# A fused attention and mixture-of-experts kernel: the first expert's weight loads, one gather and a scatter pace moved in the queue, and score units issued in pairs

## The chip, the cores and the metric

The kernel runs on one core of a Trainium2 chip. A core has a matrix engine (TensorE, PE in the profile; its weight loads are PEld), a vector engine (VectorE, DVE), a scalar engine (ScalarE, ACT), GpSimd (POOL) and a sync engine (SyncE, SP), each with its own instruction queue, and 16 DMA engines that all queues share. The metric is the time of one execution in device microseconds; several executions are timed and their median is given.

## What is computed

The reference is a block-causal attention whose output goes through a noisy top-2 router and eight experts. It is cut here to what matters.

```
q, k, v: (8, 8, 576, 64)                       # batch, heads, sequence, head size
scores = q @ k.T / 8, masked where block(i) < block(j), blocks of 64
attn   = softmax(scores) @ v                   # per batch and head
x      = attn, heads side by side              # (4608 tokens, 512)
noisy  = x @ w_gate + log(1 + exp(x @ w_noise)) * noise      # (4608, 8)
top2   = the two largest experts of each token, softmax weights of the two
for each expert e and each token that chose it:
    out[token] += weight * (relu(x[token] @ w1[e]) @ w2[e])  # 512 -> 1024 -> 512
```

## The kernel before

**Attention in units.** The eight batches are taken in four groups `g` of two batches (`NG = 4`). A group has two sets `st` of four heads, and a set is cut into 13 score units (`UN = 13`), so that a group has 26 (`UG = 26`) and the kernel 104. `score_unit(g, u)` (line 285) issues one unit: a few matmuls of K against Q into one of two PSUM buffers `sc` (line 299; the two batches of the group lie in the two halves of the 128 rows), and one ScalarE exponential of 128x1024 elements into `esc` (line 302). The thirteenth unit of a set is small (lines 310 and 313) and is followed by memsets of the masked blocks (line 316).

**The slot table.** All other work is entered by hand in a table, `at(slot, fn, ...)`, and `run(slot)` issues what stands at a slot, sorted by kind: router steps, AV tiles, transposes, then everything else in the order of entry. In the attention stage slot `u` follows unit `u`:

```
    for u in range(NG * UG):
        score_unit(*divmod(u, UG))
        run(u)
```

The slots hold: `transpose_qk` (lines 256 and 259, Q and K of this and of the next group, copied out by DVE or ACT), `av_tile` (lines 341 and 352; probabilities times V into `av`, then a reciprocal and a multiply on DVE into `xr`, lines 356 and 357), `x_transpose` (line 373), the 16 router steps of a group (lines 381 to 478, DVE mostly), loads of Q, K, V and weights, and the scatters. An AV tile has an index `idx` of 0 to 8. Indices 0 to 7 are whole 128-token blocks; index 8 holds the last 64 tokens of both batches, with five terms `jt` for each head of which the last (`jt = 4`) has 64 rows only. Slots 104 to 110 finish the last group; from slot 111 on every slot follows one step of the expert stage.

**Scatters.** `scatter(g, j)` (line 496) writes 128 rows of a group's tokens, with their routing records, to the expert's place in DRAM (`xd`, one per half; groups 0 and 1 are half 0, groups 2 and 3 half 1). A group has 18 of them, on POOL. Each also waits for the last compute instruction issued before it (`pace[-1]`), which spreads them over time. Group 0's start at slot 52, one a slot; group 1's at 78, one a slot; group 2's at 101 and group 3's at 118, five in four slots.

**POOL's queue.** POOL issues the loads of V (line 212), of Q and K (lines 202 and 207) and of weights (line 232), the scatters, the gathers and the scatters of results, in the order in which the table names them. In the built program every DMA of POOL waits for one of eight semaphores in turn, so that the ninth waits for the first to land.

**Experts.** A half's tokens for an expert are a block of 640 places; the order of the blocks `b` is `SEQ`: experts 0, 1, 2 of half 0, experts 0, 1, 2 of half 1, then the halves in turn for experts 3 to 7. `load_x(b)` (line 516, issued by SP) reads a block transposed from `xd`, after all 36 scatters of its half have landed: `load_x(0)` into `xa`, the others into one of three buffers `xg`. `layer1(b, fb)` (line 571, eight per block, ReLU at line 574) and `layer2(b, c)` (line 583, five per block) follow. Steps are ordered `layer1(b, ...)`, the first `layer1` of the next block, then `layer2(b, ...)`. Block 0 thus takes slots 111 to 124, block 1 slots 125 to 137, and `layer1(3, 0)`, the first step that needs half 1, is at slot 145. `load_x(3)` is issued after slot 138's step, `layer1(2, 1)`.

After `layer2` ACT writes the weighted result to `yd` (lines 588 and 590). For a token's second expert `gather(b, c)` (line 611, POOL) fetches the first result from `yd`, DVE adds the two (line 593), and POOL scatters the sum to `out` (line 595). Block 0 gathers nothing, block 1 has one gather, issued after `layer1(1, 2)`, at slot 126.

**Weights.** `load_w(wE, 0, k)` loads expert 0 in four pieces of 512 KB at slots 46 to 49; expert 1 comes at slots 80, 84, 88 and 92, expert 2 from slot 112 on.

Of the kernel before, what the change touches and what calls it, by code (L numbers as in the profile page):

```python
# [19 lines left out]
def kernel(  # L20
# [37 lines left out]
    LT = (0, 1, 2, 3, 3, 4, 5, 5)  # L58
    BIG = float(1 << 20)
    SET = 4  # L60
# [3 lines left out]
    UG = 2 * UN  # L64
# [32 lines left out]
    wE = main.enter_context(tc.tile_pool(name="wE", bufs=2))  # L97
# [117 lines left out]
    def v_loads(g):  # L215
        return [(load_v, g, idx) + r for idx in range(TG) for r in token_rows(g, idx)]
# [107 lines left out]
    def av_tile(g, st, idx, part=None):  # L324
        esc, esc4 = escs[(g, st)]
        vb = vt[g % 2]
        if g not in xrs:
            xrs[g] = xr_pool.tile([P, TG, DR], BF16, tag="xr", name="xr")
            nc.gpsimd.memset(xrs[g][:, :, Dm + 2 * NREC:DR], 0.0)
            nc.gpsimd.tensor_copy(xrs[g][:, :, Dm + 4:Dm + 6].bitcast(I32)[:, :, 0], tokm[:, g, :])  # L330
        xr = xrs[g]
        if part != 1:
            avs_open[idx] = av_ps.tile([P, SET, D + 1], F32, tag="av", name="av")
        av = avs_open[idx]
        for hh in (range(SET) if part is None else range(2 * part, 2 * part + 2)):
            h = st * SET + hh
            if idx < 8:
                hf, ib = divmod(idx, 4)
                for jt in range(ib + 1):
                    c = EO[jt] + (ib - jt) * P  # L340
                    nc.tensor.matmul(out=av[:, hh, :], lhsT=esc[:, hh, hf, c:c + P],  # L341
                                     rhs=vb[:, 4 * hf + jt, h, :], start=(jt == 0), stop=(jt == ib))
            else:
                for jt in range(5):
                    for hf in range(2):
                        sl = slice(64 * hf, 64 * hf + 64)
                        if jt < 4:
                            c = EO[jt] + (4 - jt) * P
                            lhsT, rhs = esc[:, hh, hf, c:c + 64], vb[:, 4 * hf + jt, h, :]
                        else:  # L350
                            lhsT, rhs = esc4[sl, hh, :], vb[sl, 8, h, :]
                        nc.tensor.matmul(out=av[sl, hh, :], lhsT=lhsT, rhs=rhs,
                                         start=(jt == 0), stop=(jt == 4))
        if part != 0:
            rden = small.tile([P, SET, 1], F32, tag="rden")
            nc.vector.reciprocal(rden, av[:, :, D:D + 1])
            ins = nc.vector.tensor_tensor(  # L357
                out=xr[:, idx, st * SET * D:(st + 1) * SET * D].rearrange("p (h d) -> p h d", h=SET),
                in0=av[:, :, 0:D], in1=rden.to_broadcast([P, SET, D]), op=ALU.mult)
            if g == NG - 1 and st == 1:  # L360
                pace.append(ins.ins.name)
# [244 lines left out]
    def gather(b, c):  # L606

        half, e = SEQ[b]
        yg = ffn["yg"][len(gathers) % GB]
        gathers.append(b)  # L610
        ins = nc.gpsimd.indirect_dma_start(  # L611
            out=yg, out_offset=None, in_=yd[half][0:e * CAP, :],
            in_offset=bass.IndirectOffsetOnAxis(ap=orows[half][:, e, c:c + 1], axis=0),
            bounds_check=e * CAP - 1, oob_is_err=False)
        tc.add_manual_dep(ins.ins, pace[-1], SYNC_DEP, reason="spreads the descriptors over time")
        ygs[(b, c)] = yg

    gathers = []
    GJ = (2, 3, 4, 6, 7)
# [3 lines left out]
    SEQ = [(0, e) for e in range(3)] + [(1, e) for e in range(3)]  # L623
# [5 lines left out]
    def at(slot, fn, *args):  # L629
        todo.setdefault(slot, []).append((fn, args))  # L630
# [94 lines left out]
    for g in range(NG):  # L725
        s0 = g * UG
        last = g == NG - 1

        for nm, ch, i in (("q", 1, 0), ("k", 1, 2), ("k", 2, 4), ("q", 2, 6), ("k", "4A", 7), ("q", "4A", 8),
                          ("q", 3, 10), ("k", 3, 12)):  # L730
            at(s0 + i, transpose_qk, g, nm, ch)
        if not last:
            for nm, ch, i in (("q", 0, 14 if g else 19), ("k", 0, 17 if g else 22), ("q", "4B", 22), ("k", "4B", 21)):
                at(s0 + i, transpose_qk, g + 1, nm, ch)
            for i, (fn, *a) in enumerate(v_loads(g + 1)):
                at(s0 + 9 + i, fn, *a)
        if g == 0:
            at(s0 + 13, load_qk, 1, (2,))
            at(s0 + 16, load_qk, 1, (3,))
        if g == 0:  # L740
            for i, t in enumerate(((0, 6, 5), (1, 5), (6, 9))):
                at(s0 + 20 + 4 * i, load_tiles, 2, "q", *t)
                at(s0 + 21 + 4 * i, load_tiles, 2, "k", *t)
        elif g == 1:
            at(s0 + 14, load_tiles, 3, "q", 0, TG)
            at(s0 + 17, load_tiles, 3, "k", 0, TG)
        for i, a in enumerate((15, 16, 17, 18, 18, 19, 20, 21, 22, 23)):
            at(s0 + a, av_tile, g, 0, *((i,) if i < 8 else (8, i - 8)))
        r0 = s0 + UG
        if not last:  # L750
            avs = (0, 1, 1, 3, 4, 4, 5, 6, 7, 8)
            xts_ = (3, 5, 7, 9, 10)
        if g < 2:
            rsl = (11, 11, 12, 13, 14, 15, 16, 17, 19, 20, 21, 22, 23, 24, 25, 26)
            r1 = 26
        elif g == 2:
            rsl = (11, 11, 12, 13, 13, 14, 15, 16, 18, 19, 19, 20, 20, 21, 22, 22)
            r1 = 23
        else:
            avs, xts_ = (0, 0, 1, 1, 2, 2, 3, 3, 4, 4), (2, 3, 4, 5, 5)  # L760
            rsl = (5, 6, 6, 7, 7, 8, 8, 9, 10, 10, 11, 11, 12, 12, 13, 13)
            r1 = 14
        for i in range(TG + 1):
            at(r0 + avs[i], av_tile, g, 1, *((i,) if i < 8 else (8, i - 8)))
        for j in range(5):
            at(r0 + xts_[j], x_transpose, g, j)
        for j in range(RSTEPS):
            at(r0 + rsl[j], router_step, g)
        for j in range(2 * TG):
            at(r0 + r1 + (j if g < 2 else 4 * j // 5), scatter, g, j)  # L770
    at(3, setup_consts)
    at(4, sort_nz, 0)
    at(8, transpose_nz, 0)
# [6 lines left out]
    at(UG + 4, clear_x, 0, UG + 3)  # L780
    at(2 * UG + 4, clear_x, 1, 2 * UG + 3)
    for k in range(4):
        at(2 * UG - 6 + k, load_w, wE, 0, k)
        at(3 * UG + 2 + 4 * k, load_w, wE, 1, k)
    for u in range(NG * UG):
        score_unit(*divmod(u, UG))
        run(u)
        if u == 3 * UG + 13:
            raws_up.close()
            ffn["x"] = raws_up.enter_context(tc.tile_pool(name="xgp", bufs=3, side="right", reuse_waits="tile"))  # L790
            ffn["rec"] = raws_up.enter_context(tc.tile_pool(name="recp", bufs=1, side="right", reuse_waits="tile"))
            wM = raws_up.enter_context(tc.tile_pool(name="wM", bufs=1, side="right", reuse_waits="tile"))
            at(3 * UG + 18, load_x, 0)
            at(3 * UG + 19, load_x, 1)
            at(3 * UG + 20, load_rec, 0)
            at(3 * UG + 21, load_x, 2)
            for k in range(4):
                at(4 * UG + (8, 10, 13, 16)[k], load_w, wM, 2, k)
# [32 lines left out]
    for fn, b, j in steps:  # L831
        fn(b, j)
        if fn is layer1:
            if (b, j) in XL:
                load_x(XL[b, j])
            if (b, j) == (2, 1):
                load_rec(1)
            if (b, j) == (3, 3):
                read_rec(1)
            if (b, j) in WL:  # L840
                load_w(*WL[b, j])
            if b < 9 and j in GJ and GJ.index(j) < LT[SEQ[b][1]]:
                gather(b, GJ.index(j))
            if 9 <= b + 1 < NB and j in GS and GS.index(j) < LT[SEQ[b + 1][1]]:
                gather(b + 1, GS.index(j))
        if fn is layer2 and 9 <= b + 1 < NB and j == 0 and LT[SEQ[b + 1][1]] > 4:
            gather(b + 1, 4)
            if b + 1 == NB - 1:
                nc.gpsimd.drain()  # L849
        run(slot)  # L850
        slot += 1
        open_top(slot)
# [8 lines left out]
    with tc.If(rs["over"] > 0):  # L861
# [16 lines left out]
        for half in range(NH):  # L878
            with tc.For_i(half * TH * P, (half + 1) * TH * P, P) as r0:
# [16 lines left out]
                for e in range(E):  # L896
# [3 lines left out]
                    for fb in range(FB):  # L900
                        hp = sc_ps.tile([P, 2, 512], F32, tag="sc")
                        for db in range(DB):
                            nc.tensor.matmul(out=hp[:, 0, 0:P], lhsT=w1sb[:, db, fb * P:(fb + 1) * P],
                                             rhs=xoT[:, db, :], start=(db == 0), stop=(db == DB - 1))
                        nc.scalar.activation(out=hsf[:, fb, :], in_=hp[:, 0, 0:P], func=AF.Relu)
                    yp = av_ps.tile([P, Dm], F32, tag="av")
                    for fb in range(FB):
                        nc.tensor.matmul(out=yp, lhsT=hsf[:, fb, :], rhs=w2sb[:, fb, :],
                                         start=(fb == 0), stop=(fb == FB - 1))
# [33 lines left out]
```

## Time and profile before

| what | value |
|---|---|
| median of 5 runs | 454.72 us (452.59 to 463.37) |
| profiled execution | 455.81 us, of which the span from the first to the last instruction is 453.9 us |
| mean granted TensorE clock | 0.946 |
| PE busy | 406.5 us, 90% |
| PEld busy | 252.9 us, 56% |
| ACT busy | 252.9 us, 56% |
| POOL busy | 249.0 us, 55% |
| DVE busy | 158.2 us, 35% |
| layer 1 and layer 2 matmuls | 134.5 + 11.6 us and 139.3 us |
| score exponentials (line 302) | 93.9 us, 96 of 1026 ns |
| scatters (line 496) | 70.9 us, 72 of 985 ns |

A group in the profile is named by line, engine and operation, with output and input tiles (buffer numbers left out). The waits view says which engine waited for what, as "engine tile line <- releaser: us in total, times, longest". The timeline lists instructions by start and duration, with the idle time of the engine before them in brackets. The windows view gives, for a stretch of the span, the busy time of each engine (with the number of instructions), the granted PE clock, the share of the 16 DMA engines (over 1 where packets overlap) and GB/s. Matmuls are pipelined, so that PE's busy time is not PE at its peak. A releaser is inferred: of several semaphores the one that came last is named, and where the engine named had long been done it was another, often a DMA.

### The profile page before, as it was taken

Reading aid. Unit: us, or ns where it says so; the run is one execution under the profiler, and the core shown is the slowest. Engines: PE = TensorE matmul, PEld = TensorE weight load, DVE = VectorE, ACT = ScalarE, POOL = GpSimd, SP = SyncE. Lnnn points to the kernel's source line nnn. Section 1 sums busy time; section 2 is a strip of 40 time slices with the busy share of each in tenths; the row PEclk is TensorE's granted clock in tenths of the full one; section 3 lists DMA queues with packets and bytes.
Section 4 is the critical chain, followed back from the end, with each engine's and each line's share of the span. In section 5 each row is a group of like instructions: output and inputs, shape, how many; then the busy total and the mean of one; then the engine's idle time right before and its main releaser. Section 6 shows DMA issues by size and latency. Waiting matters only on the chain. (4 is left out here: it accounts for less than half of the span.)

```text
span 453.9 us, 9831 instructions
## 1 busy us (share of the span) xinstructions
PE 406.5 (90%) x3936; PEld 252.9 (56%) x3952; DVE 158.2 (35%) x508; ACT 252.9 (56%) x343; POOL 249.0 (55%) x297
## 2 busy tenths in 40 slices
PE   2789978988898289997999999999999999999994
PEld 2456756756657155654556556556556556555561
DVE  1577789688687416000300110110110211212212
ACT  2899898898872034543445446455455455355240
POOL 8777644338878778671301143345543756647343
PEclk9969999989956769998999999999999999999998
DMA  8999999998968799949986786986989999924222
GB/s 135 171 122 170 222 193 186 236 207 112 120 142 181 176 258 175 239 166 163 211 167 94 164 175 125 225 189 152 244 171 206 221 222 237 240 92 168 72 85 103
DMA packets 134633, 78.67 MB, mean 173 GB/s; under 512 B 96001, under 2 KB 124419, under 8 KB 134580
## 3 DMA queue, kind: packets, MB, share of 16 engines
q0 software_dynamic: 70368, 55.78, 74.4%
q1 hardware_dynamic: 54132, 13.00, 15.1%
q10 hardware_dynamic: 10080, 9.18, 6.3%
q8 instruction: 33, 0.54, 0.5%
q14 instruction: 20, 0.16, 0.1%
HBM read 68.28 MB, written 33.13 MB: 223 GB/s over the span
## 5 line engine op out<-in xcount | busy, mean ns | idle before, releaser
L583 PE MATMUL yp<-w2sb,hq 128*128 128x512 bf16 x624 | 139.3, 380 | 1.0 <-issue 0.2
L571 PE MATMUL hp<-xg,w1sb 128*128 128x320 bf16 x960 | 134.5, 301 | 4.3 <-DMA xg<-xd 2.3
L571 PEld LDWEIGHTS <-w1sb 128*128 128x128 bf16 x1024 | 101.4, 99 | 58.6 <-DMA xa<-xd 10.5
L574 ACT ACTIVATE hq<-hp 128x640 bf16<-128x640 f32 x128 | 89.8, 703 | 74.3 <-PE hp L571 73.5
L593 DVE SCALAR_TENSOR_TENSOR yo<-yp,wrow,yg 128x512 f32<-128x512 f32 x46 | 34.5, 751 | 231.9 <-ACT ysb L588 205.6
L583 PEld LDWEIGHTS <-hq 128*128 128x128 bf16 x640 | 62.8, 98 | 73.6 <-issue 0.8
L302 ACT ACTIVATE esc<-sc 128x1024 bf16<-128x1024 f32 x96 | 93.9, 1026 | 9.7 <-PE sc L299 9.3
L496 POOL DMA_INDIRECT xd<-xr,slots x72 | 70.9, 985 | 35.4 <-issue 14.8
L588 ACT ACTIVATE ysb<-yp,wrow 128x512 bf16<-128x512 f32 x70 | 48.1, 687 | 75.8 <-PE yp L583 71.1
L611 POOL DMA_INDIRECT yg<-yd,orow x46 | 47.5, 1032 | 72.9 <-ACT hq L574 56.9
L595 POOL DMA_INDIRECT out_dram<-yo,trow x46 | 45.7, 993 | 65.0 <-DVE yo L593 50.9
L299 PE MATMUL sc<-hq 64*128 64x512 bf16 (+4 forms) x320 | 40.3, 321 | 12.3 <-ACT esc L302 11.1
L212 POOL DMA_DIRECT2D vt<-in_v_dram x40 | 34.5, 874 | 11.7 <-DMA vt<-in_v_dram 3.3
L341 PE MATMUL av<-vt,esc 128*128 128x65 bf16 x640 | 34.7, 212 | 3.0 <-DVE xr L357 2.4
L341 PEld LDWEIGHTS <-esc 128*128 128x128 bf16 x640 | 27.5, 109 | 16.1 <-DVE xr L357 7.2
L357 DVE TENSOR_TENSOR xr<-av,rden 128x256 bf16<-128x256 f32 x72 | 30.6, 425 | 2.6
L256 PE MATMUL tp<-ident,raw 128*64 128x128 bf16 x512 | 23.4, 242 | 2.8 <-DMA raw<-in_q_dram 1.7
L299 PEld LDWEIGHTS <-hq 64*128 64x128 bf16 x320 | 12.6, 96 | 20.8 <-issue 13.0
L269 ACT ACTIVATE hq<-tp 128x1024 bf16<-128x1024 bf16 (+1 forms) x20 | 17.1, 853 | 11.3 <-PE tp L259 6.0
L256 PEld LDWEIGHTS <-raw 128*64 128x64 bf16 x512 | 18.0, 122 | 7.1 <-issue 2.2
L571 PE MATMUL hp<-xa,w1sb 128*128 128x320 bf16 x64 | 11.6, 354 | 10.4 <-DMA xa<-xd 10.4
L262 DVE COPY hq<-tp 128x1024 bf16<-128x1024 bf16 (+1 forms) x24 | 14.4, 598 | 7.0 <-PE tp L256 5.6
(122 smaller groups left out, 225.7 us busy)
## 6 DMA issues: line engine op xcount, KB each, us to landing
yd<-ysb ACTq DMA_DIRECT2D x70, 128.0 KB, 4.0
w1sb<-in_moe_w_dram POOLq DMA_DIRECT2D x16, 512.0 KB
w2sb<-in_moe_w_dram POOLq DMA_DIRECT2D x16, 512.0 KB
vt<-in_v_dram POOLq DMA_DIRECT2D x32, 128.0 KB
raw<-in_q_dram POOLq DMA_DIRECT2D x9, 256.0 KB
raw<-in_k_dram POOLq DMA_DIRECT2D x9, 256.0 KB
xd<-zero SPq DMA_DIRECT2D x16, 132.0 KB, 7.7
raw<-in_q_dram POOLq DMA_DIRECT2D x1, 1152.0 KB
```

The source lines that it names most:

```text
L212: nc.gpsimd.dma_start(out=vt[g % 2][p0:p0 + n, idx, :, 0:D], in_=v[b, :, s0:s0 + n, :].rearrange("h s d -> s h d"))
L256: nc.tensor.transpose(to[64 * hf:64 * hf + 64, :, r, :], raw[:, (t0, t1)[hf], r * 64:(r + 1) * 64], ident)
L299: nc.tensor.matmul(out=sc[:, hf, off:off + z - a], lhsT=kT[sl, c0 + jt * P:c0 + jt * P + P], rhs=qT[sl, c0 + a:c0 + z], start=True, stop=True)
L302: ins = nc.scalar.activation(out=esc[:, hh, :, piece * 512:(piece + 1) * 512], in_=sc, func=AF.Exp, scale=scale)
L341: nc.tensor.matmul(out=av[:, hh, :], lhsT=esc[:, hh, hf, c:c + P], rhs=vb[:, 4 * hf + jt, h, :], start=(jt == 0), stop=(jt == ib))
L496: ins = nc.gpsimd.indirect_dma_start(out=xd[half].bitcast(I32), out_offset=bass.IndirectOffsetOnAxis(ap=slots[:, g * TG + idx, i:i + 1], a ...
L571: nc.tensor.matmul(out=hp[:, n, 0:NW], lhsT=w1sb[:, db, fb * P:(fb + 1) * P], rhs=xgs[b][:, db, n * NW:(n + 1) * NW], start=(db == 0), sto ...
L574: ins = nc.scalar.activation(out=hs[b][:, fb, :].rearrange("p (n w) -> p n w", n=2), in_=hp[:, :, 0:NW], func=AF.Relu)
L583: nc.tensor.matmul(out=yp, lhsT=hs[b][:, fb, c * P:(c + 1) * P], rhs=w2sb[:, fb, :], start=(fb == 0), stop=(fb == FB - 1))
L588: ins = nc.scalar.activation(out=ysb, in_=yp, func=AF.Copy, scale=w)
L595: ins = nc.gpsimd.indirect_dma_start(out=out, out_offset=bass.IndirectOffsetOnAxis(ap=trow[half][:, e, c:c + 1], axis=0), in_=yo, in_offse ...
L611: ins = nc.gpsimd.indirect_dma_start(out=yg, out_offset=None, in_=yd[half][0:e * CAP, :], in_offset=bass.IndirectOffsetOnAxis(ap=orows[hal ...
```

## The change

1. Expert 0's four loads move from slots 46 to 49 to slots 53, 55, 57 and 59.
2. The scatters of group 0 are issued three in two slots (slots 52 to 63). Those of group 3 are issued one a slot (slots 118 to 135), where they were five in four slots.
3. Block 1's gather is issued after `layer1(1, 1)`, one step sooner (slot 125).
4. In the attention stage units `u` and `u + 1` are issued in a row, then the table's slots `u` and `u + 1`.
5. In an AV tile of index 8 the heads 1 and 3 take their 64-row term first, where they took it last.

```diff
-        for hh in (range(SET) if part is None else range(2 * part, 2 * part + 2)):
-            h = st * SET + hh
-            if idx < 8:
...
+        else:
+            for hh in heads:
+
+                jts = (0, 1, 2, 3, 4) if hh % 2 == 0 else (4, 0, 1, 2, 3)
+                for jt in jts:
                     for hf in range(2):
...
                         nc.tensor.matmul(out=av[sl, hh, :], lhsT=lhsT, rhs=rhs,
-                                         start=(jt == 0), stop=(jt == 4))
+                                         start=(jt == jts[0]), stop=(jt == jts[-1]))
...
         for j in range(2 * TG):
-            at(r0 + r1 + (j if g < 2 else 4 * j // 5), scatter, g, j)
+            at(r0 + r1 + (2 * j // 3, j, 4 * j // 5, j)[g], scatter, g, j)
...
     for k in range(4):
-        at(2 * UG - 6 + k, load_w, wE, 0, k)
+        at(2 * UG + 1 + 2 * k, load_w, wE, 0, k)
         at(3 * UG + 2 + 4 * k, load_w, wE, 1, k)
     for u in range(NG * UG):
-        score_unit(*divmod(u, UG))
+        if u % 2 == 0:
+            score_unit(*divmod(u, UG))
+            score_unit(*divmod(u + 1, UG))
         run(u)
...
-            if b < 9 and j in GJ and GJ.index(j) < LT[SEQ[b][1]]:
+            if b == 1 and j == 1:
+                gather(b, 0)
+            elif 1 < b < 9 and j in GJ and GJ.index(j) < LT[SEQ[b][1]]:
                 gather(b, GJ.index(j))
```

More of the change, by code (lines that the diff above doesn't have):

```diff
@@ L334, in av_tile @@
         av = avs_open[idx]
-        for hh in (range(SET) if part is None else range(2 * part, 2 * part + 2)):
-            h = st * SET + hh
-            if idx < 8:
-                hf, ib = divmod(idx, 4)
+        heads = range(SET) if part is None else range(2 * part, 2 * part + 2)
+        if idx < 8:
+            hf, ib = divmod(idx, 4)
+            for hh in heads:
                 for jt in range(ib + 1):
@@ L341, in av_tile @@
                     nc.tensor.matmul(out=av[:, hh, :], lhsT=esc[:, hh, hf, c:c + P],
-                                     rhs=vb[:, 4 * hf + jt, h, :], start=(jt == 0), stop=(jt == ib))
-            else:
-                for jt in range(5):
+                                     rhs=vb[:, 4 * hf + jt, st * SET + hh, :], start=(jt == 0), stop=(jt == ib))
+        else:
+            for hh in heads:
+                jts = (0, 1, 2, 3, 4) if hh % 2 == 0 else (4, 0, 1, 2, 3)
+                for jt in jts:
                     for hf in range(2):
@@ L348, in av_tile @@
                             c = EO[jt] + (4 - jt) * P
[L349 removed]
+                            lhsT, rhs = esc[:, hh, hf, c:c + 64], vb[:, 4 * hf + jt, st * SET + hh, :]
                         else:
[L351 removed]
+                            lhsT, rhs = esc4[sl, hh, :], vb[sl, 8, st * SET + hh, :]
                         nc.tensor.matmul(out=av[sl, hh, :], lhsT=lhsT, rhs=rhs,
[L353 removed]
+                                         start=(jt == jts[0]), stop=(jt == jts[-1]))
         if part != 0:
```

## The prediction, made before the changed kernel ran

> **What bounds the kernel now.** I read the waits of PE first: busy 90% of the span, PE loses time only where it waits.
>
> ```profile
> PE hp L571 <- DMA xa<-xd: 10.4, 1, 10.4
> ...
> PE hp L571 <- DMA xg<-xd: 2.3, 1, 2.3
> ```
>
> The first is block 0's input, the second block 3's, the first input of half 1. From 215 us to the end PE waits 1.1 us in all, so whatever the change is worth must come out of what stands before `layer1(3, 0)` at 210.51 us. PE's timeline places both:
>
> ```profile
> 149.34 1.05 PE L388 MATMUL lg<-wgn,xT 128*128 128x16 bf16 x36
> 160.82 1.51 PE L571 MATMUL hp<-xa,w1sb 128*128 128x320 bf16 x5 [10.44 <-DMA xa<-xd]
> ...
> 210.51 2.31 PE L571 MATMUL hp<-xg,w1sb 128*128 128x320 bf16 x8 [2.29 <-DMA xg<-xd]
> ```
>
> Attention's last matmul ends at 150.4. Next, what the two loads waited for: SP's timeline and its waits.
>
> ```profile
> 155.01 2.62 SPq L516 DMA_TRANSPOSE xa<-xd  x1
> ...
> 204.70 2.54 SPq L516 DMA_TRANSPOSE xg<-xd  x1
> ```
>
> SP waited for scatters (xd<-xr,slots). Half 0's last scatter is POOL's 36th, half 1's the 72nd: they end at 150.35 and 202.68, 4.7 and 2.0 us before these issues, and 5.8 us lie between each issue and PE's start. So **the chain is POOL's queue**, not attention. POOL's timeline where the change works:
>
> ```profile
> 76.95 0.75 POOL L232 DMA_DIRECT2D w2sb<-in_moe_w_dram  x1 [4.39 <-DMA raw<-in_q_dram]
> 78.13 0.74 POOL L232 DMA_DIRECT2D w2sb<-in_moe_w_dram  x1 [0.43 <-DMA vt<-in_v_dram]
> 80.09 1.09 POOL L496 DMA_INDIRECT xd<-xr,slots  x1 [1.22 <-DVE rden L356]
> 81.48 1.02 POOL L496 DMA_INDIRECT xd<-xr,slots  x1 [0.30 <-issue]
> 86.82 0.97 POOL L496 DMA_INDIRECT xd<-xr,slots  x1 [4.31 <-DMA raw<-in_k_dram]
> 88.82 0.97 POOL L496 DMA_INDIRECT xd<-xr,slots  x1 [1.03 <-DMA vt<-in_v_dram]
> 92.03 0.97 POOL L496 DMA_INDIRECT xd<-xr,slots  x1 [2.25 <-ACT sp L395]
> 94.68 0.97 POOL L496 DMA_INDIRECT xd<-xr,slots  x1 [1.68 <-ACT esc L302]
> 98.52 0.97 POOL L496 DMA_INDIRECT xd<-xr,slots  x1 [2.88 <-ACT esc L302]
> 100.46 0.97 POOL L496 DMA_INDIRECT xd<-xr,slots  x1 [0.97 <-DMA xd<-xr,slots]
> ...
> 124.07 1.05 POOL L496 DMA_INDIRECT xd<-xr,slots  x1 [0.30 <-issue]
> ```
>
> The ninth DMA waits for the first: 86.82 is eight behind the K load of 69.09; 92.03, 94.68, 98.52 and 100.46 are eight behind expert 0's four pieces. ACT is named there because exponentials end all the time; I read these waits as weights landing, at about 91.7, 94.4, 98.2 and 100.2. From there POOL never rests: one scatter per 1.28 us (0.97 and 0.30 of issue), group 1's first at 124.07, 16 us later than its slot 78 (unit 78's exponential begins at 105.7). The windows say the rest:
>
> ```profile
> 54.00:99.00 45.00, 39.19 (x773) 27.79 (x774) 35.87 (x121) 40.21 (x52) 19.55 (x25) 0.96 1.46 213
> 99.00:105.00 6.00, 5.48 (x112) 3.77 (x113) 5.28 (x20) 5.66 (x8) 4.38 (x5) 1.00 0.34 123
> ```
>
> The DMA engines are full until 99 (share 1.46), then nearly idle for 6 us (0.34) while POOL works off scatters.
>
> **Part 1, weights and group 0's scatters.** In the changed order of POOL five scatters and one weight piece stand ahead of the scatter that waits for the K load, where two scatters and all four pieces stood. The slot numbers are known at 75.6 (line 476 ends at 75.8). Scatters 0 to 4 and a piece (0.75 and some 0.3 of issue) take 76 to 83, the sixth waits for K until 86.8 as now (K's load is not moved), and from there 13 scatters at 1.28, three pieces at 1.0 and ten V loads at 0.98 follow: 16.6 + 3.0 + 9.8 = 29.4, so 116.2. For waits on pieces, which stand four DMAs apart and land some 3 us apart behind K, I add 1.1. Group 1 starts at 117.3, **6.8 us sooner** than 124.07. Ends: 10.7 if POOL never waited (75.8 + 23.0 + 4.0 + 9.8 and 0.8 of memsets and gaps = 113.4), 0 if the pieces hold POOL as long as now. I take 6.8, since K's wait is the only long one in sight. Group 1 then runs as now (18 scatters and 4 pieces in 26.3 us; its slots lie 11 us ahead): half 0 ends at 143.6 and `layer1(0, 0)` starts at **154.0**, 3.6 us after attention.
>
> **Part 2, pairs and AV order.** Both end in attention, behind that 3.6 us. In each pair one change between 64-row score matmuls and full AV or transpose matmuls goes. [...] Against it: two score buffers exist, so in a pair the second unit needs the exponential just before, and ACT (93.9 us for 96) has 2 us in hand for all work of two slots. ACT's waits for scores are 9.3 us now in 26 places. Bounds: 10 us gained to 12 lost (0.6 us in five of 13 pairs, four times); I take 0, hidden, and **from a loss of 3.6 us on it counts fully**. The reordered terms (line 352, 13.7 us in all) hide there too.
>
> **Part 3, half 1.** Group 2 follows at once, and PE and POOL both stand 6.8 us earlier up to the seventh scatter of group 3. Times below are as now, to be shifted by 6.8:
>
> ```profile
> 186.25 0.97 POOL L496 DMA_INDIRECT xd<-xr,slots  x1 [1.89 <-DMA w2sb<-in_moe_w_dram]
> ...
> 191.35 1.07 POOL L611 DMA_INDIRECT yg<-yd,orow  x1 [0.30 <-issue]
> ...
> 201.71 0.97 POOL L496 DMA_INDIRECT xd<-xr,slots  x1 [0.30 <-ACT ysb L588]
> ```
>
> Now the gather stands behind ten scatters of group 3 and ahead of eight. In the new order it stands behind seven and ahead of eleven, since both edits push scatters past it, and the result scatter of block 1 (line 595, slot 133) gets ahead of the last three. The seventh scatter (186.25) is done at 187.2. The gather then waits for block 0's `yd`: the fifth store is issued at 184.18, and stores there land after 5.8 us at least, so 190.0. All eleven scatters wait in POOL's queue meanwhile. Gather, eleven scatters and one result scatter: 190.2 + 1.07 + 0.3 + 12 x 1.276 - 0.3 = 206.6, against 202.68: **3.9 us given back** (2.6 of waiting, 1.3 of the result scatter). Their paces (the last at slot 135, ACT at 197.9) are never late. Bounds: 1.3 if `yd` lands by 187.5, 5.4 at the slowest store there (7.3 us).
>
> Shifted, half 1 ends at 199.8, 2.9 us sooner, and `layer1(3, 0)` starts at 207.6. PE is ready at 208.2 - 6.8 = 201.4 and **waits 6.2 us instead of 2.3**.
>
> **The clock.** [...]
>
> ```profile
> 210.50:214.00 3.50, 3.27 (x11) 1.74 (x13) 0.00 (x0) 0.70 (x1) 0.00 (x0) 0.51 1.15 103
> ```
>
> Clock 0.51 after 2.3 us. I take the row: 0 more, 1.7 as the other end.
>
> **Sum.** 6.8 - 3.9 = 2.9 us less: 452.9 for the profiled execution (455.81, span and 1.9 us around it). It lay 1.1 us above the median; on the median's scale, 454.72 - 2.9 = **451.8 us**.
>
> **Rivals.**
> A, **POOL keeps its lead** (chance 0.28): weights land so that POOL hardly waits (9 us), and `yd`, with fewer transfers beside it, lands in the 4.0 us that its median row gives, so that half 1 gives back 1.5. For: DMA is idle at 99 to 105. Against: all five stores there took 5.8 to 7.3. Net 7.5, time 447.2.
> B, **the weights hold the scatters, and the gather holds them again** (0.11), slower: each piece now takes one of eight places among scatters, and four of these waits (about 2 to 3 us each now) stay. The gain of part 1 falls to 0, and 3.9 of the gather with a cold window of 1.7 remain: 5.6, time 460.3. It decides when part 1 brings less than 1 us. Against: the engines' 6 idle us.
> C, **pairs starve ACT** (0.11): attention ends 8 us later, at 158.4. PE, `yd`, gather and load 3 all follow: -2.4 + 3.9 = +1.5, time 456.2; at 12 us lost, 460.
> D, that the pairing does not do what it says would show in nothing, being hidden, and is part of the forecast (0.50).
>
> **Numbers.** A measurement here tells about 1%, 4.5 us, from no change. The forecast with part 1 between 4 and 9 us runs from nothing to 5 us gained: 0.15 of its 0.50 lies beyond 1% faster, 0.35 within. A is faster (0.28), B slower (0.11), C splits 0.08 within, 0.03 slower. Faster 0.43, same 0.43, slower 0.14. The range, 446.0 to 458.5, takes in A and most of C; the forecast's own is 449.5 to 455.5.
>
> **What would show.** Right: group 1's first scatter near 117, `xa`'s wait near 3.6 us, the gather on POOL with some 2.5 us idle before it, the result scatter ahead of the last three scatters, PE's wait for block 3 longer than now. Wrong: attention's end past 154; a first scatter of group 1 past 121 or before 114; block 3's wait gone; PE waits after it.

## The result, and the profile after

The changed kernel takes **452.51 us** (median of 29 runs, 448.17 to 464.20) against 454.97 us for the kernel before in the same measurement. The ratio is 0.9924, with a 95% interval of 0.9901 to 0.9946: about 0.8% faster, a step so small that the same pair measured again (e5 below) gives 0.996 with an interval that reaches 1.000. Every kernel here has some slower executions: medians count all of them, ratios and intervals only the fast ones. The forecast was 451.8 us. The profiled execution took 450.46 us (span 448.6), against 455.81 before; it lies 2.1 us below its median and the one before 0.8 us above its own, so the two profiles differ by more than the medians do.

Line numbers after are those of before plus 3 in what follows attention's AV: the scatter is L499, the transposing load L519, the expert's layers L574 and L586, the weighted store L593, the result scatter L598, the gather L614.

TensorE first, its timeline around the two places at which the kernel before waited (start, length, then in brackets the idle time and what ended it):

```profile
153.51 1.05 PE L391 MATMUL lg<-wgn,xT 128*128 128x16 bf16 x36
154.41 4.51 PE L574 MATMUL hp<-xa,w1sb 128*128 128x320 bf16 x32
...
206.63 2.31 PE L574 MATMUL hp<-xg,w1sb 128*128 128x320 bf16 x8 [8.19 <-DMA xg<-xd]
```

The wait of 10.4 us for `xa` is gone: block 0 follows attention's last matmul at once. The wait for block 3's input has grown from 2.3 to 8.2 us. It starts at 206.63 us instead of 210.51, 3.9 us sooner. The waits of TensorE over the whole run (total, times, longest) put the long waits in the same place:

```profile
PE sc L299 <- ACT esc L302: 12.2, 20, 1.6
PE hp L574 <- DMA xg<-xd: 8.2, 1, 8.2
PE av L341 <- DVE xr L360: 7.1, 16, 1.0
```

GpSimd's timeline, at the stations of the prediction's chain:

```profile
80.97 1.10 POOL L499 DMA_INDIRECT xd<-xr,slots  x1 [10.32 <-DVE rden L359]
88.40 0.98 POOL L499 DMA_INDIRECT xd<-xr,slots  x1 [0.31 <-issue]
...
116.57 1.07 POOL L499 DMA_INDIRECT xd<-xr,slots  x1 [0.30 <-issue]
...
142.02 0.97 POOL L499 DMA_INDIRECT xd<-xr,slots  x1 [0.30 <-issue]
...
179.81 0.97 POOL L499 DMA_INDIRECT xd<-xr,slots  x1 [2.77 <-ACT hq L577]
181.60 1.06 POOL L614 DMA_INDIRECT yg<-yd,orow  x1 [0.82 <-ACT hq L577]
...
193.23 0.97 POOL L598 DMA_INDIRECT out_dram<-yo,trow  x1 [0.30 <-issue]
...
197.05 0.97 POOL L499 DMA_INDIRECT xd<-xr,slots  x1 [0.30 <-ACT hq L577]
```

Group 0's first scatter is at 80.97, the sixth at 88.40, group 1's first at 116.57 and half 0's last at 142.02; the gather is at 181.60, the result scatter at 193.23 ahead of the last three scatters, and half 1's last scatter at 197.05. SyncE issues the two loads behind the two ends:

```profile
145.76 2.93 SPq L519 DMA_TRANSPOSE xa<-xd  x1
...
199.67 3.07 SPq L519 DMA_TRANSPOSE xg<-xd  x1
```

### The profile page after: what moved, and what is told of

The parts are those of the page before. It is cut to its first block, busy times and chain, and to the rows that moved or that the text cites. A ratio compares the mean times of both kernels' runs of the same rounds, so it can differ in the third digit from the quotient of the medians.

```text
span 448.6 us, 9810 instructions
## 1 busy us (share of the span) xinstructions
PE 402.2 (90%) x3936; PEld 251.6 (56%) x3952; DVE 158.3 (35%) x508; ACT 251.8 (56%) x343; POOL 249.2 (56%) x297
## 5 line engine op out<-in xcount | busy, mean ns | idle before, releaser
L574 PE MATMUL hp<-xg,w1sb 128*128 128x320 bf16 x960 | 134.4, 301 | 8.7 <-DMA xg<-xd 8.2
L586 PE MATMUL yp<-w2sb,hq 128*128 128x512 bf16 x624 | 139.2, 380 | 1.2 <-DVE yo L596 0.2
L574 PEld LDWEIGHTS <-w1sb 128*128 128x128 bf16 x1024 | 100.3, 98 | 50.7 <-DMA xg<-xd 8.5
L586 PEld LDWEIGHTS <-hq 128*128 128x128 bf16 x640 | 62.8, 98 | 73.7 <-issue 1.0
L302 ACT ACTIVATE esc<-sc 128x1024 bf16<-128x1024 f32 x96 | 92.6, 1024 | 12.9 <-PE sc L299 12.3
L499 POOL DMA_INDIRECT xd<-xr,slots x72 | 71.2, 989 | 34.3 <-issue 13.9
L614 POOL DMA_INDIRECT yg<-yd,orow x46 | 47.4, 1031 | 74.3 <-ACT hq L577 59.0
L598 POOL DMA_INDIRECT out_dram<-yo,trow x46 | 45.7, 993 | 65.4 <-DVE yo L596 51.6
L299 PE MATMUL sc<-hq 64*128 64x512 bf16 (+4 forms) x320 | 37.7, 326 | 14.3 <-ACT esc L302 12.2
L359 DVE RECIPROCAL rden<-av 128x4 f32<-128x4 f32 x72 | 13.1, 182 | 9.6 <-PE av L341 5.0
```

What stands on the lines that cost most here:

```text
L299: nc.tensor.matmul(out=sc[:, hf, off:off + z - a], lhsT=kT[sl, c0 + jt * P:c0 + jt * P + P], rhs=qT[sl, c0 + a:c0 + z], start=True, stop=True)
L302: ins = nc.scalar.activation(out=esc[:, hh, :, piece * 512:(piece + 1) * 512], in_=sc, func=AF.Exp, scale=scale)
L499: ins = nc.gpsimd.indirect_dma_start(out=xd[half].bitcast(I32), out_offset=bass.IndirectOffsetOnAxis(ap=slots[:, g * TG + idx, i:i + 1], a ...
L574: nc.tensor.matmul(out=hp[:, n, 0:NW], lhsT=w1sb[:, db, fb * P:(fb + 1) * P], rhs=xgs[b][:, db, n * NW:(n + 1) * NW], start=(db == 0), sto ...
L586: nc.tensor.matmul(out=yp, lhsT=hs[b][:, fb, c * P:(c + 1) * P], rhs=w2sb[:, fb, :], start=(fb == 0), stop=(fb == FB - 1))
L598: ins = nc.gpsimd.indirect_dma_start(out=out, out_offset=bass.IndirectOffsetOnAxis(ap=trow[half][:, e, c:c + 1], axis=0), in_=yo, in_offse ...
```

## The experiments

They ran in three groups, each kernel beside the kernel before on the same chip. Ratios are to the kernel before of the same group. The groups fell on three chips, and the chips are not alike: the kernel before took 454.9 us in the second group, as in the measurement above, but 472.4 in the first and 469.9 in the third. I call the first kind quick and the other two slow; times are compared within a group only. The profiles of the first measurement are read beside those of the second group, since the kernel before takes the same time in both.

| label | part 1 | score units | half 1's edits | chip | median, us | ratio | interval |
|---|---|---|---|---|---|---|---|
| e1_no_pairs | yes | single | both | slow | 477.32 | 1.013 | 1.005 to 1.022 |
| e2_pairs_only | no | pairs | none | slow | 475.04 | 1.012 | 1.006 to 1.018 |
| e3_weights_pace0_only | yes | single | none | slow | 471.78 | 1.002 | 0.997 to 1.007 |
| e4_half1_undone | yes | pairs | none | slow | 482.17 | 1.030 | 1.021 to 1.038 |
| e5_changed_again | yes | pairs | both | quick | 453.04 | 0.996 | 0.993 to 1.000 |
| e6_no_pairs_again | yes | single | both | quick | 455.28 | 0.997 | 0.994 to 1.001 |
| e7_weights_pace0_again | yes | single | none | quick | 445.95 | **0.981** | 0.976 to 0.986 |
| e8_half0_four_blocks | yes | pairs | both, other block order | quick | 461.02 | 1.014 | 1.010 to 1.018 |
| e9_pairs_old_half1 | yes | pairs | none | slow | 480.33 | 1.024 | 1.017 to 1.030 |
| e10_gather_only | yes | single | gather | slow | 476.86 | 1.016 | 1.009 to 1.024 |
| e11_pace3_only | yes | single | pace | slow | 476.03 | 1.010 | 1.005 to 1.014 |
| e12_w2_behind_scatters | yes | single | none, w2 moved | slow | 481.04 | 1.020 | 1.012 to 1.028 |

"Part 1" is expert 0's weight pieces and group 0's scatter pace; "half 1's edits" are the earlier gather and the new pace of group 3's scatters. The new order of the AV terms stays in all but e2.

### First group, a slow chip: the change taken apart

The edit of **e1_no_pairs**, against the changed kernel:

```diff
-        if u % 2 == 0:
-            score_unit(*divmod(u, UG))
-            score_unit(*divmod(u + 1, UG))
+        score_unit(*divmod(u, UG))
```

> The changed kernel with score units one by one again; weights, group 0's pace, gather and group 3's pace stay changed. Theory (the queue of POOL sets block 3, pairs are hidden or nearly so): attention's last router matmul ends near 150 to 151 instead of 154.5, PE then waits 1 to 3 us for xa, group 1's first scatter comes at 115 to 118, block 3's first matmul at 205 to 207, PE waiting 6 to 9 us for it; time within 1.5 us of the changed kernel, some 2 to 3.5 us under the kernel before. Rival (pairs lengthen attention by 4 us and this passes to the end): block 3 starts 3 to 4 us sooner than 206.6, time 5.5 to 7 us under the kernel before.

**e2_pairs_only** is the kernel before with the same three lines the other way round.

> The kernel before with score units in pairs and nothing else. Theory (hidden): attention ends between 148 and 155, PE's wait for xa is 160.8 less that end (6 to 12 us), xa and block 3 start within 1 us of 160.8 and 210.5; time within 1 us of the kernel before. Rival (pairs keep PE's clock low and slow every group): attention ends 3 to 5 us late with granted clock 0.5 in windows of set 2 of group 1 as in the changed kernel, group 0's scatters start later, and the time is 2 to 4 us over the kernel before.

**e3_weights_pace0_only** is the kernel of e1 with half 1's edits undone as well:

```diff
-            at(r0 + r1 + (2 * j // 3, j, 4 * j // 5, j)[g], scatter, g, j)
+            at(r0 + r1 + (2 * j // 3, j, 4 * j // 5, 4 * j // 5)[g], scatter, g, j)
...
-            if b == 1 and j == 1:
-                gather(b, 0)
-            elif 1 < b < 9 and j in GJ and GJ.index(j) < LT[SEQ[b][1]]:
+            if b < 9 and j in GJ and GJ.index(j) < LT[SEQ[b][1]]:
```

> The changed kernel with single score units, the gather at its old step and group 3 at its old pace: what is left is expert 0's weights between the scatters, group 0's faster pace and the order of terms in AV tiles of index 8. Theory (part 1 brings 6.8 us, half 1's edits give back 3.9 of it): group 1's first scatter at 115 to 118, gather behind ten scatters of group 3 and without idle time of over 0.5 us before it, half 1's last scatter 6 to 7.5 us sooner than 202.7, block 3 at 203 to 205; time 5.5 to 7 us under the kernel before. Rival (the gather's place costs nothing, POOL waits there for a weight piece anyway): block 3 at 206 to 207, time as the changed kernel, 2 to 3.5 us under the kernel before.

**e4_half1_undone** has the second of these diffs and keeps the pairs.

> The changed kernel with pairs, but the gather at its old step and group 3 at its old pace. Theory: attention ends as in the changed kernel (152 to 155), the result scatter of block 1 comes after all scatters again, so half 1's last scatter is 1.3 to 3 us sooner than 198.0 and block 3 starts 1.3 to 3 us sooner than 206.6; time 1.5 to 3 us under the changed kernel. Rival: no difference, or 1 us over it because block 1's second layer waits for the later gather.

What each measured stands in the table: e1 1.013, e2 1.012, e3 1.002, e4 1.030. Nothing is faster than before here, part 1 is worth nothing, and the pairs cost 1.2% on the kernel before and 2.8 points on top of part 1 (e4 less e3). Of the texts put on record for this group only the rival of e2 named what happened in kind, a low clock between 64 and 67 us (0.62); it put the loss at 2 to 4 us, and 1.2% is 5.7. Why part 1 is worth nothing stands in the profile of e3. First TensorE's end of attention and start of block 0, then SyncE's issue of the load that block 0 needs:

```profile
169.94 1.05 PE L391 MATMUL lg<-wgn,xT 128*128 128x16 bf16 x36
170.85 2.33 PE L574 MATMUL hp<-xa,w1sb 128*128 128x320 bf16 x16
```

```profile
148.02 2.52 SPq L519 DMA_TRANSPOSE xa<-xd  x1
```

The load is issued 22.8 us before block 0 starts, where 5.8 to 7 us lie between the two when TensorE waits for it. **On this chip attention is the chain** and GpSimd's queue is not: what part 1 gains is hidden, and what the pairs lose is paid. No wait for an `xg` stands among TensorE's waits in these profiles either. The exponentials show what is slower. Their row in the groups by line (busy, mean ns, idle time before them), first e3, then the same kernel on the quick chip (e7):

```profile
L302 ACT ACTIVATE esc<-sc 128x1024 bf16<-128x1024 f32 x96 | 93.9, 1025 | 22.2 <-PE sc L299 11.4 <-remote 4.7 <-PE av L341 3.6
```

```profile
L302 ACT ACTIVATE esc<-sc 128x1024 bf16<-128x1024 f32 x96 | 93.6, 1028 | 9.1 <-PE sc L299 8.8
```

The instruction takes the same 1.03 us on both; the idle time ahead of it is 22.2 instead of 9.1 us, part of it ended by what the profile calls remote. Such pauses appear from 72 us on. What they are stays open: no experiment tested it.

This does not account for half 1's edits here: e1 stands 1.1 points above e3, though no wait for an `xg` shows in either. The pauses go on among the experts and differ from profile to profile. The longest wait of TensorE among e1's experts is one for ScalarE, which itself stood 4.93 us for what is called remote; at the same place in e3 it stood 0.80:

```profile
222.25 0.70 ACT L577 ACTIVATE hq<-hp 128x640 bf16<-128x640 f32 x1 [4.93 <-remote]
223.00 8.62 PE L574 MATMUL hp<-xg,w1sb 128*128 128x320 bf16 x48 [6.32 <-ACT hq L577]
```

So the 1.1 points are not shown to be a cost of the queue.

This group lacked the changed kernel itself. The second group has it as a control.

### Second group, the quick chip: the same kernels with a control

**e5_changed_again** is the changed kernel, unedited.

> The changed kernel itself, as the control that its ablations lacked: the first four experiments ran on a chip on which the kernel before took 472.4 us instead of 454.7, and the changed kernel was not among them. Theory (the change is worth about 0.8% and does not depend on the chip): ratio 0.990 to 0.996 to the kernel before. Rival (the pairs cost what the fourth experiment showed, and the first chip hid it): ratio 1.01 to 1.03, as slow as or slower than the same kernel without pairs, if this chip is of the slower kind.

Measured: 0.996, at the upper end of what the theory gave; the interval overlaps that of the first measurement. The rival is out on this chip. Its profile repeats the first one: group 1's first scatter at 115.42, no wait for `xa`, 8.8 us for block 3.

**e6_no_pairs_again** has the edit of e1.

> The changed kernel with single score units, as in the first experiment, now beside the changed kernel. Theory (pairs are hidden behind nothing any more, cost attention the 3 us of one slow set by chance only): within 1 us of the changed kernel; the clock of 0.5 between 62 and 80 us appears or not without regard to the pairs. Rival (pairs make TensorE wait for the second unit's exponential, and the waits drop the clock): 2 to 4 us faster than the changed kernel, attention ending near 150.5 instead of 154.5, and PE waiting for xa again for about 1 us, because the scatters then end last.

Measured: 455.28 us, ratio 0.997 beside 0.996, so the pairs make no difference that can be told *in the company of half 1's edits*. The rival put the wait for `xa` at about 1 us and the theory named none; it is 6.2 us, since attention ends 3.7 us sooner than in e5 and the load is issued 3.4 us later (148.34 against 144.97). The theory's other clause, that a clock of 0.5 appears between 62 and 80 us with or without pairs, was wrong: in e6 it is 1.00 from 57 to 79 us.

**e7_weights_pace0_again** has the edit of e3.

> Expert 0's weight pieces and group 0's scatters as in the changed kernel, everything else as before. Theory (half 1's edits, the earlier gather and the faster pace of group 3, cost what the gather's place takes: 1.5 to 3 us): 1.5 to 3 us faster than the no-pairs kernel of this call, last scatter of half 1 that much sooner, and a wait for block 3's input that is shorter by as much. Rival (the queue of POOL is full to the last scatter, so that the order within it is free): the same as the no-pairs kernel within 0.5 us.

Measured: 445.95 us, 1.9% faster than before and some 7 us faster than the changed kernel. The theory was right in kind and far too small: 1.5 to 3 us were expected between e6 and e7, the ratios differ by 1.7%, 7.6 us. TensorE in e7:

```profile
146.53 1.05 PE L391 MATMUL lg<-wgn,xT 128*128 128x16 bf16 x36
153.67 6.06 PE L574 MATMUL hp<-xa,w1sb 128*128 128x320 bf16 x32 [6.08 <-DMA xa<-xd]
...
202.44 1.26 PE L574 MATMUL hp<-xg,w1sb 128*128 128x320 bf16 x8 [2.31 <-DMA xg<-xd]
```

Block 3 starts at 202.44, 8.1 us sooner than before, and the span is 9.4 us shorter. Now GpSimd's gather, last scatter and result scatter in e7, and the same places with half 1's edits, in e6:

```profile
183.10 1.07 POOL L614 DMA_INDIRECT yg<-yd,orow  x1 [0.30 <-issue]
...
193.44 0.97 POOL L499 DMA_INDIRECT xd<-xr,slots  x1 [0.31 <-ACT ysb L591]
194.72 0.97 POOL L598 DMA_INDIRECT out_dram<-yo,trow  x1 [0.30 <-issue]
```

```profile
178.50 0.97 POOL L499 DMA_INDIRECT xd<-xr,slots  x1 [1.06 <-ACT ysb L591]
185.55 1.06 POOL L614 DMA_INDIRECT yg<-yd,orow  x1 [6.07 <-ACT hq L577]
...
197.16 0.97 POOL L598 DMA_INDIRECT out_dram<-yo,trow  x1 [0.30 <-DMA yd<-ysb]
...
200.99 0.97 POOL L499 DMA_INDIRECT xd<-xr,slots  x1 [0.30 <-issue]
```

In e7 ten scatters of group 3 stand ahead of the gather, so `yd` has landed when GpSimd gets there, and the result scatter comes behind the last scatter. In e6 GpSimd is done with what stands ahead of the gather 3.3 us sooner and waits 6.07 us there, with eleven scatters behind it. e6's last scatter starts 7.55 us later: 5.8 of it is the gather's longer wait, 1.3 the result scatter, 1.7 a later start of group 1, and 1.1 less is lost at the scatter before (2.16 us in e7). Since the profiled execution of e6 is one of its longer ones (457.9 us, against a median of 455.3), I read the kind of the loss from these lines, and its size from the ratios.

**e8_half0_four_blocks** is the changed kernel with other blocks first:

```diff
-    SEQ = [(0, e) for e in range(3)] + [(1, e) for e in range(3)]
-    for e in range(3, E):
+    SEQ = [(0, e) for e in range(4)] + [(1, e) for e in range(4)]
+    for e in range(4, E):
...
-                    WL[3 + 2 * i + k // 2, (2, 6)[k % 2]] = (pool, 3 + i, k)
+                    WL[(3 if i else 1) + 2 * i + k // 2, (2, 6)[k % 2]] = (pool, 3 + i, k)
...
-    XL = {(2, 1): 3, (2, 2): 4}
+    XL = {(1, 1): 3, (2, 1): 4}
...
-            if (b, j) == (2, 1):
+            if (b, j) == (3, 1):
                 load_rec(1)
-            if (b, j) == (3, 3):
+            if (b, j) == (4, 3):
                 read_rec(1)
```

> The changed kernel with one block more of half 0 ahead of half 1 (experts 0 to 3 of half 0, then 0 to 3 of half 1), so that the input of half 1 is needed one block later; expert 3's weights are loaded two blocks sooner for it, four pieces more in POOL's queue ahead of the last scatters. Theory (the 8.2 us wait for block 3's input is the whole of what part 1 did not bring to the end): 6 to 8.5 us faster than the changed kernel, no wait of TensorE above 1 us for an xg. Rival (the weights of expert 3 come late, or their pieces hold the last scatters by 6 us or more, and the wait returns at block 4): within 2 us of the changed kernel, with a wait on w1sb at block 3 or on xg at block 4.

Measured: 461.02 us, 8 us slower than the changed kernel. The theory had the wait right and the time wrong: TensorE waits for no `xg`, but loses more just behind it, in block 2's second layer, a place that neither text named:

```profile
208.80 3.38 PE L586 MATMUL yp<-w2sb,hq 128*128 128x512 bf16 x8 [4.42 <-DVE yo L596]
219.93 4.96 PE L586 MATMUL yp<-w2sb,hq 128*128 128x512 bf16 x16 [7.75 <-DVE yo L596]
```

The two gathers of block 2 are issued at 202.3 and 203.7, behind the scatters and the moved pieces (198.3 and 199.7 in the changed kernel), and `yo` waits for their landing, the second until 219.1, with TensorE behind it. In the changed kernel TensorE reaches this second layer only at 208.74, after its wait of 8.2 us for block 3. Taking that wait away is not worth 8 us, because **the gathers in the same queue are next**. The edit moves the order of blocks and expert 3's pieces together; how much of the late landing is due to the pieces is not shown.

### Third group, a slow chip again

**e9_pairs_old_half1** is the kernel of e4.

> The changed kernel with its pairs, but the first gather at its old step and group 3's scatters at the old pace. Theory (half 1's edits carry the whole loss against the kernel with part 1 alone, and the pairs' 3 to 4 us at attention's end are covered by the wait for xa): ratio to the kernel before 0.979 to 0.987, as the kernel with part 1 alone (0.981), last scatter of half 1 near 195.5 us, TensorE's wait for block 3 longer than 2.3 us. Rival (the pairs lose what the fourth experiment seemed to show, 2.8%): ratio 1.00 or above, attention ending past 158 us.

**e10_gather_only** is e3 with the earlier gather alone, **e11_pace3_only** e3 with the new pace of group 3 alone: one each of the two halves of e3's diff taken back.

> Part 1 and the earlier first gather; single units, group 3's scatters at the old pace. Theory (the gather waits on POOL for block 0's yd with scatters queued behind it): the gather is reached near 181.8, yd lands near 184 to 185.5, so 2 to 4 us of idle POOL before it; half 1 ends that much later than with part 1 alone, ratio 0.984 to 0.991. Rival (only the result scatter that gets ahead of the last scatters costs, and that comes with the pace): the same as part 1 alone within 0.3%, idle below 1 us.

> Part 1 and the new pace of group 3's scatters (one a slot); single units, the first gather at its old step. Theory (the pace pushes scatters past the gather and one result scatter ahead of the last ones): the gather is reached near 180.5 to 181.8 and waits for yd to 184 to 185.5, and one result scatter (1.28 us) stands ahead of the last three: 3 to 5 us later than part 1 alone, ratio 0.987 to 0.992. Rival (the pace only spreads scatters that had to wait anyway): 1.3 us, ratio 0.982 to 0.985.

**e12_w2_behind_scatters**, against e3:

```diff
-                at(4 * UG + (8, 10, 13, 16)[k], load_w, wM, 2, k)
+                at(4 * UG + (8, 10, 27, 27)[k], load_w, wM, 2, k)
```

> Part 1 alone, and the two pieces of expert 2's second weight issued behind half 1's last scatter instead of among group 3's scatters. Theory (POOL's queue ends half 1, and the two pieces take 2 us of it and make the fifth scatter wait 2.2 us): last scatter 3 to 4 us sooner than with part 1 alone, block 3's wait gone, 2 to 3 us faster, ratio 0.974 to 0.978, unless the pieces come late for block 2's second layer, which starts near 203 us: they issue near 191 to 192 and have some 11 us. Rival (the store yd that the gather needs is what sets the queue from there): the gather waits as much as the pieces cost, and the time is that of part 1 alone within 0.3%.

Measured: 1.024, 1.016, 1.010 and 1.020. The numbers expected were those of the quick chip, and they are not tested by these. As far as they go: e9 repeats e4 (2.4 and 3.0% slower), so the pairs with part 1 are slower than the kernel before on both slow chips; each of half 1's edits alone is slower than before too. The single kernel that would set both apart, e3, was not in this group. In e10 GpSimd waits 4.55 us before the gather, but 3.44 in e3 on the other slow chip, so it cannot simply be put down to the edit. In e12 the last scatter came no sooner than in e3 on the other slow chip (213.2 against 213.6 us), and TensorE waited 5.4 us for `yo` behind a late gather, as in e8; on the quick chip it was not run.

## Why the prediction came out right, step by step

**What bounds the kernel: right for this chip, and only there.** On the quick chip the end follows the start of block 3: before 210.51, changed 206.63 and 206.28 (e5), e7 202.44; from there to the end of the span lie 243.4, 242.0, 244.4 and 242.1 us. On the slow chips no wait for an `xg` shows, and attention sets when the experts start.

**Part 1: right.** Group 1's first scatter was put at 117.3; it came at 116.57, and at 115.42 and 115.30 in e5 and e7. The way there held for the kernel that has part 1 alone: in e7 the first scatter is at 76.18 and the sixth waits for the K load until 86.49 (86.8 predicted). With pairs the first one is only at 80.97, because the slots' work comes later, and the sixth finds K landed. Both ways end at the same place. The 1.1 us added for pieces on their way was not needed. `layer1(0, 0)` was put at 154.0, and came at 153.67 in e7. Its worth at block 3 is 8.1 us there (with the order of the AV terms), against 6.8 put in the sum. One reading was off without harm: from the beginning of unit 78's exponential (105.7) to group 1's first scatter (124.07) lie 18.4 us, not 16.

**Part 2: the size was off, and the sum survived it.** "I take 0, hidden" named what happens in a pair (two score buffers, so that the second unit needs the exponential just before) and a point, 3.6 us, from which it counts. The point was right, the 0 was not. Attention's last matmul ends at 152.7 to 154.6 us in the three paired kernels of the quick chip (changed, e5, e8), and at 147.6 to 150.4 in the single ones (before, e6, e7): **about 4 us lost**, just past that point. On the slow chips it is 175.2 to 181.4 (e2, e4, e9) against 169.7 to 172.4 (e1, e3, e10, e11, e12). One place recurs: between 57 and 79 us one set (four heads of two batches) takes 16.2 to 18.5 us, from one last exponential to the next, in the six paired kernels (changed, e2, e4, e5, e8, e9), and 15.0 to 15.3 in the single ones. TensorE there, changed kernel and then e7:

```profile
61.49 0.39 PE L299 MATMUL sc<-hq 64*128 64x512 bf16 x2 [1.05 <-ACT esc L302]
62.41 0.45 PE L299 MATMUL sc<-hq 64*128 64x64 bf16 x4 [0.52 <-ACT esc L302]
```

```profile
59.80 0.40 PE L299 MATMUL sc<-hq 64*128 64x320 bf16 x4 [1.01 <-ACT esc L302]
60.13 0.30 PE L341 MATMUL av<-vt,esc 128*128 128x65 bf16 x4
60.72 0.39 PE L299 MATMUL sc<-hq 64*128 64x512 bf16 x2 [0.28 <-ACT esc L302]
```

In the pair nothing stands between the two waits, 1.05 and 0.52 us; in single units an AV group does, and the second wait is 0.28. The granted clock differs as well. The windows of the changed kernel, then of e7 (busy time of PE, PEld, DVE, ACT, POOL, granted clock, DMA share, GB/s):

```profile
61.00:64.00 3.00, 1.64 (x19) 0.91 (x19) 2.78 (x11) 3.00 (x4) 0.93 (x2) 0.77 1.49 192
64.00:67.00 3.00, 3.00 (x43) 2.06 (x41) 2.19 (x10) 1.55 (x3) 2.51 (x5) 0.50 2.38 156
```

```profile
61.00:64.00 3.00, 2.80 (x62) 2.04 (x60) 2.76 (x14) 3.00 (x4) 1.73 (x4) 1.00 1.58 189
64.00:67.00 3.00, 2.21 (x34) 1.32 (x36) 2.80 (x10) 2.75 (x5) 2.14 (x4) 1.00 2.43 159
```

TensorE is busy 1.64 of 3 us, and the clock of the next 3 us is 0.50: it is busy all of them with 43 matmuls, while ACT, busy 2.75 us there in e7, gets 1.55. So the pairs don't only wait: behind the waits stands a clock of 0.50, where e7 has 1.00. From 61 to 64 us TensorE is busy 1.34 to 1.83 us in all six paired kernels, on either kind of chip, and the clock of the next 3 us is 0.50 to 0.78. In all eight single ones it is busy 2.43 to 2.80 us, and the clock stays at 1.00. The order of the AV terms is not the reason: e2 has the old one and a clock of 0.62, e3 and e7 have the new one and 1.00. The 10 us put down as the most that the pairs could gain are shown by no run: the AV matmul takes 212 ns in the changed kernel as before, the score matmul 326 against 321. These means hold the stretch at 0.50 too, so a small gain elsewhere is not excluded.

**What covered it: luck.** The loss is paid back by something that no line of the prediction names. Attention's late end leaves TensorE no wait for `xa`, and it enters the experts at a clock of 1.00 (154.40 to 158.95 us): 32 matmuls in 4.51 us, where e7 needs 6.06 behind a wait of 6.08, and before 7.14 behind 10.44, at 0.63 (160.80 to 168.00). Block 0 and its fifth store of `yd` (which the gather needs) in e5, then in e6, the same kernel without pairs:

```profile
152.70 4.51 PE L574 MATMUL hp<-xa,w1sb 128*128 128x320 bf16 x32
172.16 0.33 ACTq L593 DMA_DIRECT2D yd<-ysb  x1
```

```profile
155.37 7.45 PE L574 MATMUL hp<-xa,w1sb 128*128 128x320 bf16 x32 [6.20 <-DMA xa<-xd]
178.26 0.33 ACTq L593 DMA_DIRECT2D yd<-ysb  x1
```

The store comes 6.1 us sooner with pairs: 2.7 because block 0 starts sooner, 2.9 because its first 32 matmuls take 4.51 us and not 7.45 (clock 0.50 in e6 from 155.40 to 158.80), and the rest behind it. The gather waits 0.8 and 0.3 us in the two profiles of the changed kernel, and 6.07 in e6. So with these pairs **the early gather finds its `yd` landed**. I read this as the reason why e5 and e6 take the same time though attention differs by 3.7 us; the kernel that would test it, pairs without half 1's edits, did not run on the quick chip. Why the load of `xa` is issued later without pairs is not shown either.

**Part 3: right in kind.** The gather behind seven scatters, the result scatter ahead of the last three, and the longer wait at block 3 all came. Half 1's last scatter ends 4.7 us sooner than before where 2.9 were forecast: 2.7 us given back of the 7.4 that half 0's end had gained, and not 3.9, since of the 2.6 us of waiting for `yd` only 0.8 came (`yd` was early, as above). Without the pairs the same step was too small: 5.8 us of waiting. Block 3 was put at 207.6 and came at 206.63; the wait was put at 6.2 and is 8.2, since TensorE got there sooner (198.4 instead of 201.4).

**Its own signs: mixed.** Of the signs of being right, group 1's first scatter, the result scatter and block 3's longer wait came; a wait of 3.6 us for `xa` and 2.5 us of idle GpSimd before the gather did not (0 and 0.82). One sign of being wrong came as well: attention ended past 154, at 154.56 (152.85 in e5). The number was right with two of its terms, the pairs and the gather's wait, missed in opposite directions.

**The clock at block 3: the row was right.** 8 matmuls take 2.31 us behind the wait of 8.19, at a clock of 0.59, as they did behind 2.29 before, at 0.51:

```profile
206.60:210.00 3.40, 3.24 (x12) 1.75 (x14) 0.00 (x0) 0.70 (x1) 0.00 (x0) 0.59 1.17 109
```

But the row was not a law: e7 waits 2.31 us and the 8 matmuls take 1.26 us, at a clock of 1.00:

```profile
202.40:205.90 3.50, 3.46 (x19) 1.88 (x20) 0.00 (x0) 1.14 (x2) 0.00 (x0) 1.00 1.11 104
```

The two waits of 2.3 us differ in what followed them (granted clock 0.51 before, 1.00 in e7), so the length of the single wait did not decide it alone; what else did is not shown. The 1.7 us put as the other end, about what 3.5 us at 0.51 lose against 1.00 (an estimate from the row), did not come on top of what was lost before.

**The sum.** Forecast 2.9 us less, measured 2.5 in the medians and 5.3 in the profiled spans. The terms at block 3 were -6.8 and +3.9; measured they are -8.1 (e7) and +4.2 (changed less e7). Of that 4.2, 1.3 is a later start of group 1, 1.3 the result scatter, 0.5 the gather, 0.6 a weight piece's place in the queue and 0.6 a later landing (each read to 0.1 us). Rival C named what the pairs do and overpriced it, at 8 us, for the quick chip, where it is about 4; between e4 and e3 attention's ends differ by 10.4. A and B did not come.

What stays open: the pauses on the first and third groups' chips, what half 1's edits cost there, what each of the two costs on the quick chip, and part 1 with pairs but without half 1's edits on the quick chip.

## What to carry to other kernels

A change of several edits can be right in sum and still hold a loss: here part 1 alone is faster than all of it (0.981 against 0.996 in one group), because the other edits hold up the queue that part 1 had eased: a gather and a result scatter now stand ahead of the last scatters. Before an instruction that waits is moved forward in an in-order queue, count what stands behind it, and ask whether its producer moves forward as well. And a cover is a property of the chip that was profiled: where attention ended 23 us later (e3 against e7), the same saving was worth nothing, and the "hidden" pairs made the kernel 1.2% slower (e2).

## What the runs showed of the hardware that was not expected

- The same kernel (e7 and e3) takes 446.0 us on one chip and 471.8 on another, with equal instruction times (the exponential 1.03 us on both) and more idle time between them (22.2 instead of 9.1 us before the exponentials). The kernel before takes 454.9 us on the first, and 472.4 and 469.9 on two others.
- Short waits stood ahead of a clock of about a half, as a long one did (8.19 us, then 0.59): two waits of 1.05 and 0.52 us with little between them, TensorE busy 1.64 of 3 us, went ahead of 3 us at a clock of 0.50. All six paired kernels show the like there (busy at most 1.83, clock at most 0.78), and none of the eight single ones does (busy at least 2.43, clock 1.00).
- A single wait of 2.3 us was followed by a clock of 0.51 in one kernel and of 1.00 in another.
